# Layer 2's double pairs: the sum that frees a PSUM place is put ahead of the older pair's differences

## The chip, the core and the metric

The kernel runs on one core of a Trainium2 chip. The core has five engines that follow their own instruction queues in order: TensorE (PE, matrix products into PSUM; PEld loads its weights), VectorE (DVE), ScalarE (ACT), GpSimd (POOL) and SyncE (SP, which here only issues DMAs). They wait for each other through semaphores. The metric is the device time of one execution in microseconds (us), the median of several runs.

## What is computed

```python
def _attn_ref(x, w_r, w_i, b_r, b_i):          # x: (2, 3008, 256)
    X = np.fft.rfft(x, axis=1)
    Xr, Xi = X.real, X.imag
    Yr = Xr @ w_r - Xi @ w_i + b_r
    Yi = Xr @ w_i + Xi @ w_r + b_i
    Yr = np.sign(Yr) * np.maximum(np.abs(Yr) - lam, 0.0)
    Yi = np.sign(Yi) * np.maximum(np.abs(Yi) - lam, 0.0)
    return np.fft.irfft(Yr + 1j * Yi, n=x.shape[1], axis=1)

x = _attn_ref(...).reshape(6016, 256)
h = x @ w_in1;  x = (h / (1 + np.exp(-h))) @ w_out1        # layer 1, 256 -> 2048 -> 256
h = x @ w_in2;  y = np.maximum(0.01 * h, h) @ w_out2       # layer 2, 256 -> 2048 -> 256
```

Everything is float32. The spectral part comes first and is no subject here.

## The kernel before, in words

The 6016 tokens stand in the free dimension, in 12 chunks of 512 (the last has 384). Each fp32 operand of a matrix product is split into a high part of fewer bits and a low remainder, and a product is three matmuls (high by low, low by high, high by high). So every value that PE is to read next costs a cast on ACT (the high part, `high`, names `h`, `ha`, `hb`) and a subtraction on DVE or POOL (the remainder, `low`, names `l`, `la`, `lb`).

The 2048 hidden features are 16 blocks of 128, two to a **pair**, 8 pairs p = 0..7 to a chunk. A pair's first product (256 -> 2 x 128 features) goes to PSUM, is activated, and goes through a second product into the accumulators `acc`. The second product uses a scheme with seven instead of eight block products, for which differences of the activated blocks are needed: `t1` (POOL), `t23` and `t4` (DVE).

In layer 2, in chunks 2 to 10 (`FAST`), the odd pairs use such a scheme for the first product too: `unit` computes seven products 1 to 7 of 256 columns in two PSUM places `a` and `b`, one after another. What a place holds is copied away by ACT (`keep`) or summed by DVE with a kept part (`join`) before the next product uses the place again. Product 7 begins `b` anew, so it must wait until the first `join` has read `b`.

An even pair `pr` and the odd pair `fa` behind it are worked on together by `both_pairs`, a **double pair**: 4 to a chunk (p = 0, 2, 4, 6), 36 in all. The order of the calls in `both_pairs` is the order of the instructions in each engine's queue; no scheduler changes it. A double pair also finishes the pairs before it: `one` is the `fa` of the double pair before, `two` its `pr`. PE's order is `pr.first(0)`, products 1 and 2, `pr.first(1)`, products 6 and 7, `two`'s second product in parts "1" and "a", products 5 and 4, `two`'s part "b", product 3, and `one`'s three parts, of which "b" reads `hb` and `lb` of `one`. `make_next` inserts one step of work for the next chunk's input: in p = 0 a load, in p = 2 its split (`xhi`, `xlo`), in p = 4 four sums (`xsum`, two on POOL, then two on DVE), in p = 6 their split (`xs`). At a chunk's end (in p = 0, for the chunk before) `finish` joins the accumulators, with five sums on DVE and two on POOL.

The lines that the texts name: 582 `first`; 599 `activate`; 619 `unit`; 624 `keep`; 627 `join`; 645 `low`; 657 `t1`; 664 `t23`; 671 `t4`; 683 `high`; 690 the second product; 479 `sums_x2`; 751 to 756 `finish`. The sum in question and the two differences:

```python
        def join(self, at_, src, key):
            nc.vector.tensor_tensor(out=quarter(self.f1, at_), in0=self.ph[src], in1=self.ph[key], op=ALU.add)
...
                nc.vector.tensor_tensor(out=v[:, 3:5], in0=b22, in1=v[:, 0:2], op=ALU.subtract)
...
                nc.vector.tensor_tensor(out=u[:, 1280:], in0=u[:, 1024:1280], in1=b2[:, 256:], op=ALU.subtract)
```

`b2` is in PSUM for an even pair and in SBUF (`f1`) for an odd one; `u`, the casts and the kept parts are in SBUF. `high("b")` and `low("b")` of a pair need its `t23` and `t4`; `high("a")` and `low("a")` need its `t1`.

Of the kernel before, what the change touches and what calls it, by code (L numbers as in the profile page):

```python
# [80 lines left out]
def spectral_mlp_kernel(ctx, tc, x, w_r, w_i, b_r, b_i, w_in1, w_out1, w_in2, w_out2, da, ea, dm, out):  # L81
# [695 lines left out]
    def make_next():  # L777
        if todo and (make := todo.pop(0)):
            make()

    def both_pairs(i):

        two, one, pr, fa = pairs[i - 2:i + 2]
        one.high("1")
        one.low("1")
        one.t23()
        pr.first(0)
        one.t4()
        pr.activate(0)
        pr.t1()  # L790
        fa.unit(1, 2)
        fa.keep("p1", "a")
        fa.join(2, "b", "p1")
        one.high("a")
        one.low("a", nc.gpsimd)
        pr.first(1)
        one.high("b")
        one.low("b")
        pr.activate(1)
        fa.unit(6, 7)  # L800
        fa.keep("u2", "a")
        fa.keep("p7", "b")
        two.products("1")
        pr.t23()
        pr.t4()
        two.products("a")
        pr.high("1")
        pr.high("a")
        pr.low("a", nc.gpsimd)
        fa.unit(5, 4)  # L810
        fa.join(1, "a", "p7")
        fa.join(0, "b", "u2")
        pr.low("1")
        if pr.p != 4:
            make_next()
        two.products("b")
        pr.high("b")
        pr.low("b")
        fa.unit(3)
        fa.activate_fast()  # L820
        fa.t1()
        if pr.p == 4:
            make_next()
        for which in "1ab":
            one.products(which)
        one.finish(0)
        one.finish(1)

    for i in range(len(pairs) + 2):
        if i < len(pairs) and (pairs[i].fast or i + 1 < len(pairs) and pairs[i + 1].fast):  # L830
            if not pairs[i].fast:
                if pairs[i].p == 0 and (k := phases.index((2, pairs[i].c)) + 1) < len(phases):
                    todo = ahead(*phases[k])
                both_pairs(i)
            continue
        pr = pairs[i] if i < len(pairs) else None
        one, two = blocks(i - 1), blocks(i - 2)
# [114 lines left out]
```

## Time and profile before

| | |
|---|---|
| median of 3 runs | 1213.45 us (1213.26 to 1213.97) |
| the profiled execution | 1213.22 us, its span 1211.2 us |
| mean granted clock of TensorE | 0.975 |
| busy, share of the span | PE 97%, DVE 71%, ACT 67%, POOL 54% |
| layer 2's 36 double pairs | 742.20 to 1169.40 us of the span |

The span runs from the first to the last instruction. PE's matmuls are pipelined, so a row's duration overlaps the next row; the distance of the starts is what a matmul costs. The granted clock is what the throttle lets TensorE have, as a share of full speed. An idle time in brackets is that of the engine just before the instruction, with what ended it.

### The profile page before, as it was taken

How to read it: one execution, taken by the hardware profiler on the slowest of the kernel's cores; microseconds unless marked ns; L12 is line 12 of the kernel's file. 1: busy time of each engine (PE TensorE's matmuls, PEld its weight loads, DVE VectorE, ACT ScalarE, POOL GpSimd, SP SyncE). 2: the span in 40 equal slices, each digit the busy share in tenths (PEclk: the TensorE clock that was granted, in tenths of full speed). 3: DMA queues.
4: the chain of work that ended last, by engine and by line, in shares of the span. 5: the costliest groups of instructions: out<-in, count | busy, mean ns of one | idle time of the engine just before them, and what ended most of it. 6: DMA issues, size and time to landing. Idle time of an engine off the chain costs nothing.

```text
span 1211.2 us, 21096 instructions
## 1 busy us (share of the span) xinstructions
PE 1169.0 (97%) x7608; PEld 1078.7 (89%) x7608; DVE 860.8 (71%) x1484; ACT 814.4 (67%) x1720; POOL 649.7 (54%) x683
## 2 busy tenths in 40 slices
PE   9999999999999999999999999899899989998998
PEld 9898988889999999999999998888888878888898
DVE  4888865556667666666657788787878787878773
ACT  4888776666666666666657776566666666665674
POOL 0668656534445454544536777565655555555542
PEclk9999999999999999999999999899989999998999
DMA  9445541011121111111101010000100010000000
GB/s 237 123 136 161 157 128 58 13 49 50 35 61 57 40 57 49 47 44 45 36 1 35 32 35 23 32 19 18 35 19 18 18 35 19 18 19 31 19 1 31
DMA packets 36185, 61.80 MB, mean 51 GB/s; under 512 B 3953, under 2 KB 16081, under 8 KB 36081
## 3 DMA queue, kind: packets, MB, share of 16 engines
q1 hardware_dynamic: 35792, 60.28, 16.5%
q8 instruction: 60, 0.98, 0.4%
q14 instruction: 45, 0.36, 0.1%
q10 hardware_dynamic: 288, 0.18, 0.0%
HBM read 41.83 MB, written 18.61 MB: 50 GB/s over the span
## 4 chain that ended last, share of the span: by engine, by line
PE 81%; DVE 9%; ACT 4%; issue 4%; POOL 2%; ACTq 0%; POOLq 0%
PE acc L690 33%; PE ph L582 28%; PE pz L332 5%; PE ph L619 5%; DVE u L664 3%; PE py L361 3%; PE pa L284 2%; PE px L444 2%; DVE l L645 2%; PE pb L384 1%; ACT ha L683 1%; DVE xsum L479 1%; POOL u L657 1%; ACT u L631 1%; DVE f L627 1%
## 5 line engine op out<-in xcount | busy, mean ns | idle before, releaser
L645 POOL TENSOR_TENSOR la<-u,ha 128x512 fp32r<-128x512 f32 (+1 forms) x176 | 230.5, 1310 | 242.5 <-ACT ha L683 242.2
L645 DVE TENSOR_TENSOR lb<-u,hb 128x768 fp32r<-128x768 f32 (+1 forms) x176 | 199.5, 1133 | 191.3 <-ACT hb L683 190.9
L582 PE MATMUL ph<-xhi,winhi 128*128 128x512 f32 (+1 forms) x624 | 188.2, 382 | 0.0
L582 PE MATMUL ph<-xlo,winhi 128*128 128x512 f32 (+1 forms) x624 | 187.9, 381 | 0.0
L582 PE MATMUL ph<-xhi,winlo 128*128 128x512 f32 (+1 forms) x624 | 187.2, 380 | 0.0
L683 ACT CAST hb<-u 128x768 fp32r<-128x768 f32 (+1 forms) x176 | 141.2, 802 | 62.1 <-DVE u L671 59.2
L657 POOL TENSOR_TENSOR u<-u 128x256 f32<-128x256 f32 x160 | 146.6, 916 | 59.5 <-PE ph L619 23.6
L690 PE MATMUL acc<-hb,wlo 128*128 128x256 f32 (+1 forms) x496 | 137.9, 278 | 0.0
L690 PE MATMUL acc<-hb,whi 128*128 128x256 f32 (+1 forms) x496 | 137.6, 277 | 0.0
L690 PE MATMUL acc<-lb,whi 128*128 128x256 f32 (+1 forms) x496 | 137.6, 277 | 0.0
L582 PEld LDWEIGHTS ph<-xhi,winhi 128*128 128x128 f32 x624 | 116.4, 187 | 21.7
L582 PEld LDWEIGHTS ph<-xlo,winhi 128*128 128x128 f32 x624 | 116.4, 187 | 21.3 <-POOL xlo L467 0.3
L683 ACT CAST ha<-u 128x512 fp32r<-128x512 f32 (+1 forms) x176 | 109.0, 619 | 8.6 <-PE acc L690 7.2
L683 ACT CAST h<-ph 128x512 fp32r<-128x512 f32 (+1 forms) x140 | 80.3, 573 | 48.8 <-DVE u L671 30.2
L582 PEld LDWEIGHTS ph<-xhi,winlo 128*128 128x128 f32 x624 | 104.5, 187 | 9.6 <-ACT u L599 0.2
L597 ACT ACTIVATE ph<-ph 128x512 f32<-128x512 f32 (+1 forms) x112 | 64.7, 577 | 63.8 <-PE ph L582 63.8
L690 PE MATMUL acc<-ha,wlo 128*128 128x256 f32 (+1 forms) x352 | 104.0, 295 | 0.0
L690 PE MATMUL acc<-la,whi 128*128 128x256 f32 (+1 forms) x352 | 103.7, 295 | 0.0
L690 PE MATMUL acc<-ha,whi 128*128 128x256 f32 (+1 forms) x352 | 102.8, 292 | 0.0
L690 PE MATMUL acc<-h,wlo 128*128 128x256 f32 (+1 forms) x336 | 99.5, 296 | 0.0
L690 PE MATMUL acc<-h,whi 128*128 128x256 f32 (+1 forms) x336 | 98.3, 293 | 0.0
L690 PE MATMUL acc<-l,whi 128*128 128x256 f32 (+1 forms) x336 | 98.3, 292 | 0.0
(157 smaller groups left out, 3088.5 us busy)
## 6 DMA issues: line engine op xcount, KB each, us to landing
wraw<-in_moe_w_in_dram SPq DMA_DIRECT2D x32, 256.0 KB
wraw<-in_moe_w_out_dram SPq DMA_DIRECT2D x32, 256.0 KB
scr<-bo SPq DMA_DIRECT2D x48, 128.0 KB
scr<-x2o SPq DMA_DIRECT2D x22, 256.0 KB
x2i<-scr SPq DMA_DIRECT2D x22, 256.0 KB
out_dram<-x2o SPq DMA_DIRECT2D x22, 256.0 KB
dmr<-in_dm_dram SPq DMA_DIRECT2D x34, 160.0 KB
bt<-scr SPq DMA_DIRECT2D x14, 384.0 KB
```

The costliest lines, as they stand in the source:

```text
L284: nc.tensor.matmul(pa[h][:, s * 128:(s + 1) * 128], lhsT=xt[c][:, s, h * 128:(h + 1) * 128], rhs=da_sb, start=True, stop=True, skip_group_ ...
L332: nc.tensor.matmul(turned(pz), lhsT=u[:, h, :], rhs=turned(v[:, h].rearrange("p g e -> p (g e)")), start=(n == 0), stop=(n == len(terms) - 1))
L361: nc.tensor.matmul(turned(py), lhsT=u, rhs=turned(v), start=False, stop=(n == len(terms) - 1), skip_group_check=True)
L444: nc.tensor.matmul(px[:, s * PAIR:(s + 1) * PAIR], lhsT=bt[:, s, h * 128:(h + 1) * 128], rhs=ea_sb, start=True, stop=True, skip_group_chec ...
L582: nc.tensor.matmul(turned(ph), lhsT=u[:, h, f % HALF * 128:][:, :128], rhs=turned(v[:, h, :]), start=(i == 0), stop=(i == len(terms) - 1))
L597: nc.scalar.activation(out=out, in_=ph, func=ACTF.Silu)
L619: nc.tensor.matmul(turned(self.ph[dst]), lhsT=u, rhs=turned(m), start=(begin and i == 0), stop=(i == 2), skip_group_check=True)
L645: eng.tensor_tensor(out=lo, in0=src, in1=hi.bitcast(F32), op=ALU.subtract)
L657: nc.gpsimd.tensor_tensor(out=blk(1), in0=blk(0), in1=blk(2), op=ALU.subtract)
L664: nc.vector.tensor_tensor(out=v[:, 3:5], in0=b22, in1=v[:, 0:2], op=ALU.subtract)
L683: nc.scalar.copy(hi, src)
L690: nc.tensor.matmul(turned(dst), lhsT=u, rhs=turned(v), start=(begin and self.p == 0 and i == 0), stop=(end and self.p == NF // 2 - 1 and i ...
```

## The change

Four calls in `both_pairs` for the older pair `one` (`t23`, `t4`, `high("b")`, `low("b")`) move to later places; nothing is added or dropped.

```diff
         two, one, pr, fa = pairs[i - 2:i + 2]
         one.high("1")
         one.low("1")
-        one.t23()
         pr.first(0)
-        one.t4()
         pr.activate(0)
         pr.t1()
         fa.unit(1, 2)
         fa.keep("p1", "a")
         fa.join(2, "b", "p1")
+        one.t23()
+        one.t4()
         one.high("a")
         one.low("a", nc.gpsimd)
         pr.first(1)
-        one.high("b")
-        one.low("b")
         pr.activate(1)
         fa.unit(6, 7)
         fa.keep("u2", "a")
         fa.keep("p7", "b")
+        one.high("b")
         two.products("1")
         pr.t23()
         pr.t4()
@@
         fa.unit(5, 4)
         fa.join(1, "a", "p7")
         fa.join(0, "b", "u2")
+        one.low("b")
         pr.low("1")
         if pr.p != 4:
             make_next()
```

On DVE the rows of a double pair with p = 2 read so in the kernel before, from `low("1")` of `one` to `low("b")` of `pr` (`f_` and `l_`, `h_` with a number are the tiles `f1`, `l1`, `h1`; `ph` is PSUM; `kept` is what `keep` copied):

```order
L645 TENSOR_TENSOR l_12659<-f_12577,h_12658 128x512
L664 TENSOR_TENSOR u<-f_12577,u 128x512
L671 TENSOR_TENSOR u<-u,f_12577 128x256
L627 TENSOR_TENSOR f_12722<-ph,kept 128x256
L645 TENSOR_TENSOR lb<-u,hb 128x768
L664 TENSOR_TENSOR u<-ph,u 128x512
L671 TENSOR_TENSOR u<-u,ph 128x256
L627 TENSOR_TENSOR f_12722<-ph,kept 128x256 x2
L645 TENSOR_TENSOR l_12717<-ph,h_12716 128x512
L467 TENSOR_TENSOR xlo<-x2i,xhi 128x512
L645 TENSOR_TENSOR lb<-u,hb 128x768
```

and in the changed kernel, at the same place of the queue:

```order
L645 TENSOR_TENSOR l_12659<-f_12575,h_12658 128x512
L627 TENSOR_TENSOR f_12720<-ph,kept 128x256
L664 TENSOR_TENSOR u<-f_12575,u 128x512
L671 TENSOR_TENSOR u<-u,f_12575 128x256
L664 TENSOR_TENSOR u<-ph,u 128x512
L671 TENSOR_TENSOR u<-u,ph 128x256
L627 TENSOR_TENSOR f_12720<-ph,kept 128x256 x2
L645 TENSOR_TENSOR lb<-u,hb 128x768
L645 TENSOR_TENSOR l_12715<-ph,h_12714 128x512
L467 TENSOR_TENSOR xlo<-x2i,xhi 128x512
L645 TENSOR_TENSOR lb<-u,hb 128x768
```

The first `join` moved up by two rows, and the first `lb` (that of `one`) moved down by five, behind the two later joins. On ACT the rows of a double pair in the kernel before, from `activate(0)` to `high("b")` of `pr`:

```order
L599 ACTIVATE u<-ph 128x2x256
L624 COPY kept<-ph 128x256
L683 CAST ha<-u 128x512
L683 CAST hb<-u 128x768
L599 ACTIVATE ph<-ph 128x512
L624 COPY kept<-ph 128x256 x2
L683 CAST h_12571<-ph 128x512
```

and in the changed kernel:

```order
L599 ACTIVATE u<-ph 128x2x256
L624 COPY kept<-ph 128x256
L683 CAST ha<-u 128x512
L599 ACTIVATE ph<-ph 128x512
L624 COPY kept<-ph 128x256 x2
L683 CAST hb<-u 128x768
L683 CAST h_12569<-ph 128x512
```

The cast `hb` of `one` moved down behind `activate(1)` and the two copies. The rows of PE and POOL keep their order.

## Rows read from the trace of the kernel before

**Rows 1.** The page, busy time of each engine over the span.

```profile
PE 1169.0 (97%) x7608; PEld 1078.7 (89%) x7608; DVE 860.8 (71%) x1484; ACT 814.4 (67%) x1720; POOL 649.7 (54%) x683
```

**Rows 2.** The waits of PE: us in total, times, longest us.

```profile
PE ph L619 <- DVE f L627: 37.4, 18, 2.4
```

**Rows 3.** Windows: us, busy us of PE, PEld, DVE, ACT, POOL; granted clock; DMA.

```profile
742.20:1169.40 427.20, 389.71 (x2702) 368.82 (x2701) 341.15 (x476) 277.72 (x569) 239.19 (x197) 0.93 0.06 22
...
902.60:906.30 3.70, 3.68 (x18) 3.68 (x19) 2.07 (x3) 2.18 (x6) 0.77 (x1) 0.54 0.00 0
```

**Rows 4.** PE's timeline: start, duration, instruction; starts of double pairs, and line 619.

```profile
746.88 0.61 PE L619 MATMUL ph<-xs,ws 128*128 128x256 f32 x3 [0.44 <-DVE f L627]
...
896.44 0.63 PE L582 MATMUL ph<-xhi,winlo 128*128 128x512 f32 x2
...
902.62 1.01 PE L619 MATMUL ph<-xs,ws 128*128 128x256 f32 x3 [2.24 <-DVE f L627]
...
910.48 0.61 PE L582 MATMUL ph<-xhi,winlo 128*128 128x512 f32 x2
...
913.85 0.85 PE L619 MATMUL ph<-xs,ws 128*128 128x256 f32 x6
...
919.43 0.28 PE L690 MATMUL acc<-lb,whi 128*128 128x256 f32 x1
...
920.35 0.60 PE L582 MATMUL ph<-xhi,winlo 128*128 128x512 f32 x2
...
926.48 1.01 PE L619 MATMUL ph<-xs,ws 128*128 128x256 f32 x3 [2.23 <-DVE f L627]
...
934.38 0.60 PE L582 MATMUL ph<-xhi,winlo 128*128 128x512 f32 x2
...
944.38 0.60 PE L582 MATMUL ph<-xhi,winlo 128*128 128x512 f32 x2
```

**Rows 5.** DVE's timeline from a double pair with p = 2 on.

```profile
896.85 0.75 DVE L751 TENSOR_TENSOR x2o<-x2o,acc 128x256 f32<-128x256 f32 x2 [0.68 <-ACT x2o L747]
...
898.51 1.18 DVE L645 TENSOR_TENSOR l<-f,h 128x512 fp32r<-128x512 f32 x1
899.61 1.76 DVE L664 TENSOR_TENSOR u<-f,u 128x512 f32<-128x512 f32 x1
901.40 0.83 DVE L671 TENSOR_TENSOR u<-u,f 128x256 f32<-128x256 f32 x1
902.15 0.41 DVE L627 TENSOR_TENSOR f<-ph,kept 128x256 f32<-128x256 f32 x1
903.13 1.05 DVE L645 TENSOR_TENSOR lb<-u,hb 128x768 fp32r<-128x768 f32 x1 [0.56 <-ACT hb L683]
...
916.61 0.75 DVE L627 TENSOR_TENSOR f<-ph,kept 128x256 f32<-128x256 f32 x2
...
935.70 0.68 DVE L664 TENSOR_TENSOR u<-f,u 128x512 f32<-128x512 f32 x1
```

**Rows 6.** ACT's timeline in the same double pair.

```profile
902.27 0.83 ACT L683 CAST hb<-u 128x768 fp32r<-128x768 f32 x1 [2.80 <-DVE u L671]
```

**Rows 7.** POOL's timeline in that double pair, and around the start of p = 6.

```profile
899.10 1.72 POOL L756 TENSOR_TENSOR x2o<-x2o,u 128x512 f32<-128x512 f32 x1
900.78 1.17 POOL L657 TENSOR_TENSOR u<-u 128x256 f32<-128x256 f32 x1
901.91 1.45 POOL L645 TENSOR_TENSOR la<-u,ha 128x512 fp32r<-128x512 f32 x1
...
917.99 1.28 POOL L645 TENSOR_TENSOR la<-u,ha 128x512 fp32r<-128x512 f32 x1 [3.16 <-ACT ha L683]
919.37 1.31 POOL L657 TENSOR_TENSOR u<-u 128x256 f32<-128x256 f32 x1
920.64 1.42 POOL L479 TENSOR_TENSOR xsum<-x2i 128x256 f32<-128x256 f32 x2
...
922.61 0.79 POOL L657 TENSOR_TENSOR u<-u 128x256 f32<-128x256 f32 x1 [0.55 <-ACT u L599]
```

## The prediction

> **What bounds the kernel now.** I read the page first: the matmul engine PE is busy for 97% of the span [rows 1], so time can only come out of what PE loses. The list of PE's waits has one entry of weight: PE stands at line 619 for a DVE instruction of line 627, 18 times, 37.4 us together [rows 2]. Line 627 is `join`, the sum that reads PSUM place `b` before product 7 may overwrite it. Then I read PE's timeline [rows 4]. All the waits lie in layer 2's 36 double pairs, which run from 742.20 to 1169.40, 427.2 us [rows 3]. I count times in a double pair from the start of its `first(0)`, written +x. Two hindered ones start at 896.44 and 920.35 and last 14.04 and 14.03; two unhindered ones start at 910.48 and 934.38 and last 9.87 and 10.00, mean 9.94. 36 x 9.94 = 357.8, so 69.4 us are lost. The first double pair waits 0.44 us and costs 1.1; the other 17 cost 4.0 each. A chunk has four double pairs, p = 0, 2, 4, 6. Hindered are p = 2 (behind the five DVE sums of `finish`; 9 chunks) and p = 6 (behind the two DVE sums of `sums_x2`; 8 chunks, since the last fast chunk has none).
>
> Why 4.0, when PE idles 2.24? After the wait PE runs from 902.60 to 906.30 at a granted clock of 0.54, close to the lower of its levels (1.2 GHz), against 0.93 over all double pairs [rows 3]; 3.7 x 0.46 = 1.7 us more. The wait of 0.44 us at 746.88 was followed by matmuls at the usual pace [rows 4].
>
> Next, DVE and POOL side by side [rows 5, 7]. In p = 2 the DVE queue before `join` is: sums of `finish` from 896.85, `low("1")` to 899.69, `t23` to 901.37, `t4` to 902.23, `join` from 902.15; product 7 starts 0.47 after that, at 902.62. `t23` takes 1.76 here and 0.68 at 935.70. The ends explain it: POOL's line 756 ends at 900.82, DVE's `t23` at 901.37, POOL's `t1` at 901.95, DVE's `t4` at 902.23, POOL's `la` at 903.36, DVE's `lb` at 904.18. DVE instructions with both inputs in SBUF and POOL instructions run strictly in turns. A turn lasts 0.55 (512 columns), 0.28 (256) or 0.82 (768) on DVE, and 0.58 (256) or 1.13 (512) on POOL. For DVE instructions with a PSUM input I assume that they take no turn; the two joins from 916.61 show no stretch.
>
> The Trainium skill (SBUF — State Buffer, section Who interferes with whom) says the same: a DVE instruction with two SBUF inputs and a POOL instruction that reads SBUF exclude each other through one shared read port, for the whole instruction. It speaks against the full gain: by unhindered DVE durations the sum would be 1145, by turns 1173 (both worked out below from rows). The trace agrees, to about 0.1 us.
>
> **The change, part by part.** No instruction is added or dropped; PE's and POOL's orders stay, and no DMA moves. On DVE `join` comes ahead of `t23` and `t4` of `one`, and `lb` of `one` goes behind the two later joins. On ACT the copy `hb` of `one` goes behind `activate(1)` and two `keep`s; before, ACT stood 2.80 us for `t4` in front of it [rows 6], and `activate(1)` and the `keep`s, which PE's product 5 and DVE's differences need, stood behind it. They no longer wait for DVE, so ACT's edit costs nothing.
>
> p = 2: up to `low("1")` everything is as before, so `join` runs at +3.17 (899.61) in place of +5.71, and product 7 could start at +3.64. Its unhindered place is +3.7 (six matmuls from 913.85, in a double pair from 910.48). The wait goes. `t23` had to wait for POOL's line 756 until 900.82 anyway, so the 0.41 of `join` lies under that and `t4` still ends at +5.79. The two differences of `pr` (1.1 together, then 0.75 for the two joins at 916.61) bring DVE to +7.5, and `lb` of `one` to +8.36. PE's first matmul that reads it stands at +8.95 (919.43), so 0.6 us remain. The new wait costs nothing under that cover; without it, 1 us per us.
>
> From there I carry the turns forward. `la` of `pr` 9.49, DVE's `xlo` 10.06, POOL's `xlo` 11.19, `lb` of `pr` 12.01, `t1` of `fa` 12.59, `low("1")` of the next 13.16. The next double pair, p = 4, began at 9.94, so `low("1")` ends at its +3.2 and `join` starts in time, with only 0.1 to spare.
>
> p = 4: `t1` +3.8, `t23` +4.35, `la` +5.5, `t4` +5.8, differences +6.85, joins +7.5, `lb` of `one` +8.4. `la` of `pr` follows the last difference by 1.3 us now (joins 916.61, `la` 917.99), so it gets the turn after: 9.5; `lb` of `pr` 10.35; `t1` of `fa` 10.9. That is +0.97 of p = 6. Now it ends at 920.68, +0.33 [rows 7]. So DVE and POOL arrive 0.6 us late at `sums_x2`, because the stall in p = 2 no longer lets them catch up.
>
> p = 6: now the POOL sums end at 922.06, 1.38 after that `t1`; then both DVE sums get their turns before POOL's next `t1` (its row starts at 922.61), and `low("1")` gets its turn behind that `t1`, ahead of `la`. 0.6 later, the POOL sums end at +2.35, one DVE sum +2.65, `t1` +3.25, the second DVE sum +3.55, `la` +4.7, `low("1")` +5.25. `join` starts at +5.17 and product 7 at +5.65, where now it is +6.13 (926.48). The point is 0.45 us: had p = 4 ended that much earlier, `low("1")` would come before `la`, and the wait would fall to about 0.3.
>
> After such a stall p = 0 begins clean, as p = 0 and p = 4 do now. So I take: p = 2 saves 9 x 4.0 = 36, p = 6 saves 8 x 0.5 = 4. Does PE still slow down after an idle time of 1.7? Bounds: the 0.44 us wait did not slow it, waits of 2.0 and more did; 1.7 is nearer to these, so I take the slow clock; without it another 8 x 1.7 = 14 go. Against the profiled execution's 1213.22 (0.2 below the median) the sum is 1213.2 - 40 = 1173.
>
> **Rivals.** (1) *Both waits go.* The turns are then shorter, or PE is slower by half a microsecond per chunk, so that `low("1")` in p = 6 precedes `la`. For: 0.45 us decides, over a chain of some 25 instructions. Against: each turn is one of the trace's. 1213.2 - 68 = 1145, with left-over waits of up to 0.8 per chunk 1152.
>
> (2) *DVE paces every double pair.* DVE is busy 341.15 of 427.2 us, 9.48 per double pair, and PE needs 9.94; POOL's share would rise from 0.56 (239.19) to some 0.64 in the shorter time, and the turns lost with it. For: only 0.46 us per double pair is left. Against: part of the 9.48 is the stretch in the stalls themselves. With 0.5 us lost per double pair 1145 + 18 = 1163, with the slow clock in half of the chunks' places about 1190.
>
> (3) *Slower.* `lb` of `one` now ends at 904.18, some 5 us before PE reads it at the end of that double pair (910.48 less 1.0), and after the change 0.6 us before. If POOL takes one more turn ahead of it (1.13), PE waits 0.5 in each of 36, 18 us, not enough. If it loses two turns, w = 1.7 and PE waits 61 us: 1213 - 40 + 61 = 1234, and more with the slow clock. It decides from w = 1.1 (40 / 36). Queued behind it on DVE are `low("1")`, `xlo` and `lb` of `pr`, and `fa`'s first activation, which now writes a buffer that `lb` of `one` must have read. Against: POOL has nothing ready between +5.5 and +8.4.
>
> (4) *It does not do what it says*: `join` waits for something else than its place in the queue, and the time stays at 1213. Against: at 902.15 it starts 0.08 before `t4` ends, back to back, while PE had products 1 and 2 behind it, and product 6 too, by 900.38 (902.62 less the 2.24 of idle time).
>
> **How the numbers follow.** A measurement of this kernel tells 0.2%, 2.4 us. Forecast (the wait goes from p = 2 and stays in p = 6): 0.52, own range 1158 (no slow clock) to 1181 (p = 6 as long as now and small waits). Rival 1: 0.22, 1145 to 1158. Rival 2: 0.15, 1160 to 1195. Rival 4, or a wait that only moves: 0.05. Slower: 0.06. The range 1146 to 1186 leaves out about 2 in 10. Faster by over 0.2%: 0.52 + 0.22 + 0.15 + 0.01 = 0.90; within: 0.04; slower: 0.06.
>
> **What would show it.** In the list of PE's waits the entry at line 619 falls from 18 to about 8, all in p = 6, some 1.7 us each; p = 2 lasts 9.9 to 10.1; in p = 2 `join` ends before `t23`. In p = 4 `t1` of `fa` ends about 1.0 after the next `first(0)`, and in p = 6 POOL's `la` comes before `low("1")`. ACT's 2.80 us wait before `hb` is gone or no longer holds `activate(1)`. A clock below 1 is left only behind p = 6. I am wrong if no wait is left (rival 1), if PE waits at line 690 for `lb` (rival 3), or if p = 2 still stalls.

## The result, and the profile after

The changed kernel takes 1161.36 us (median of 4 runs, 1160.87 to 1161.74) against 1213.68 for the kernel before in the same comparison: a ratio of 0.9569 [0.9552, 0.9586], 52 us less. The forecast was 1173 with a range of 1146 to 1186. The profiled execution lasts 1160.99 us, its span 1159.0.

The page of the changed kernel, engines, answering to [rows 1]:

```profile
PE 1141.4 (98%) x7608; PEld 1052.2 (91%) x7608; DVE 867.5 (75%) x1484; ACT 816.7 (70%) x1720; POOL 668.5 (58%) x683
```

PE's waits, answering to [rows 2]:

```profile
PE ph L619 <- DVE f L627: 12.7, 8, 1.6
```

Windows, with the columns of [rows 3]: the 36 double pairs, then the 3.7 us behind one of the eight waits that are left:

```profile
742.09:1117.22 375.13, 362.38 (x2702) 342.66 (x2701) 348.51 (x476) 279.99 (x569) 257.55 (x197) 1.00 0.08 25
903.57:907.27 3.70, 3.70 (x32) 3.70 (x32) 3.24 (x7) 2.74 (x6) 0.35 (x1) 1.00 0.08 32
```

The double pairs shrank from 427.20 to 375.13 us. That is 52.1 of the 52.2 us by which the span shrank; next to nothing came or went elsewhere. Eighteen waits became eight. The granted clock over the double pairs rose from 0.93 to 1.00, and behind the wait that ends at 903.57 it is 1.00 too, where behind the one of 902.62 in [rows 3] it was 0.54.

PE's timeline of one chunk, answering to [rows 4]: the starts of p = 2, 4, 6, 0 and 2, product 7 in p = 2 and p = 6, and the first read of `lb` of `one` in p = 2:

```profile
878.01 0.60 PE L582 MATMUL ph<-xhi,winlo 128*128 128x512 f32 x2
...
881.46 0.85 PE L619 MATMUL ph<-xs,ws 128*128 128x256 f32 x6
...
887.22 0.28 PE L690 MATMUL acc<-lb,whi 128*128 128x256 f32 x1
...
888.14 0.61 PE L582 MATMUL ph<-xhi,winlo 128*128 128x512 f32 x2
...
898.08 0.62 PE L582 MATMUL ph<-xhi,winlo 128*128 128x512 f32 x2
...
903.57 0.63 PE L619 MATMUL ph<-xs,ws 128*128 128x256 f32 x3 [1.58 <-DVE f L627]
...
909.90 0.40 PE L582 MATMUL ph<-xhi,winlo 128*128 128x512 f32 x1
...
919.87 0.60 PE L582 MATMUL ph<-xhi,winlo 128*128 128x512 f32 x2
```

The lengths follow from the starts: p = 2 lasts 10.13 (before 14.04), p = 4 9.94, p = 6 11.82 (before 14.03), p = 0 9.97. In p = 2 products 6 and 7 run on as one group of six matmuls, without idle time. In p = 6 the wait is still there, 1.58 in place of 2.23, and the matmuls behind it run at the usual pace (0.63 for three; 1.01 in [rows 4]).

DVE's timeline from p = 2 to p = 6 of that chunk, answering to [rows 5]:

```profile
880.05 1.19 DVE L645 TENSOR_TENSOR l<-f,h 128x512 fp32r<-128x512 f32 x1
881.17 0.41 DVE L627 TENSOR_TENSOR f<-ph,kept 128x256 f32<-128x256 f32 x1
881.50 1.43 DVE L664 TENSOR_TENSOR u<-f,u 128x512 f32<-128x512 f32 x1
882.96 0.84 DVE L671 TENSOR_TENSOR u<-u,f 128x256 f32<-128x256 f32 x1
...
885.44 0.95 DVE L645 TENSOR_TENSOR lb<-u,hb 128x768 fp32r<-128x768 f32 x1
...
889.99 1.22 DVE L645 TENSOR_TENSOR l<-f,h 128x512 fp32r<-128x512 f32 x1
...
899.68 1.81 DVE L479 TENSOR_TENSOR xsum<-x2i,xsum 128x256 f32<-128x256 f32 x2 [1.33 <-POOL xsum L479]
901.42 1.75 DVE L645 TENSOR_TENSOR l<-f,h 128x512 fp32r<-128x512 f32 x1
903.10 0.41 DVE L627 TENSOR_TENSOR f<-ph,kept 128x256 f32<-128x256 f32 x1
```

ACT's cast `hb` of `one` in p = 2, answering to [rows 6], and POOL's timeline around the start of p = 6, answering to [rows 7]:

```profile
883.84 0.84 ACT L683 CAST hb<-u 128x768 fp32r<-128x768 f32 x1 [1.04 <-DVE u L671]
```

```profile
897.52 1.43 POOL L657 TENSOR_TENSOR u<-u 128x256 f32<-128x256 f32 x1
898.91 1.44 POOL L479 TENSOR_TENSOR xsum<-x2i 128x256 f32<-128x256 f32 x2
900.36 0.86 POOL L657 TENSOR_TENSOR u<-u 128x256 f32<-128x256 f32 x1
901.18 1.45 POOL L645 TENSOR_TENSOR la<-u,ha 128x512 fp32r<-128x512 f32 x1
```

Counted from the starts of the double pairs: in p = 2 `join` starts at +3.16 (forecast +3.17), `t4` ends at +5.79 (+5.79), `lb` of `one` ends at +8.38 (+8.36) and is first read at +9.21. `low("1")` of p = 4 ends at +13.20 (+13.16). In p = 6 `t1` of `fa` ends at +0.87 (+0.97; before +0.33), POOL's `la` gets its turn ahead of `low("1")`, `join` starts at +5.02 (+5.17) and product 7 at +5.49 (+5.65).

So two things need an answer: why eight waits of 1.6 us are not followed by a slow clock, and what the three parts of the edit did, since the prediction gave the gain to one of them.

### The profile page after: what moved, and what is told of

The parts are those of the page before. It is cut to its first block, busy times and chain, and to the rows that moved or that the text cites. A ratio compares the mean times of both kernels' runs of the same rounds, so it can differ in the third digit from the quotient of the medians.

```text
span 1159.0 us, 21096 instructions
## 1 busy us (share of the span) xinstructions
PE 1141.4 (98%) x7608; PEld 1052.2 (91%) x7608; DVE 867.5 (75%) x1484; ACT 816.7 (70%) x1720; POOL 668.5 (58%) x683
## 4 chain that ended last, share of the span: by engine, by line
PE 82%; DVE 9%; issue 4%; POOL 2%; ACT 2%; DMA 0%; SPq 0%; ACTq 0%; POOLq 0%
PE acc L690 33%; PE ph L582 31%; PE pz L332 6%; PE ph L619 4%; PE py L361 3%; PE px L444 2%; PE pa L284 2%; DVE u L664 2%; DVE l L645 2%; PE pb L384 1%; DVE f L627 1%; POOL u L657 1%; DVE lb L645 1%; POOL la L645 1%; DVE xsum L479 1%
## 5 line engine op out<-in xcount | busy, mean ns | idle before, releaser
L645 POOL TENSOR_TENSOR la<-u,ha 128x512 fp32r<-128x512 f32 (+1 forms) x176 | 245.4, 1395 | 199.7 <-ACT ha L683 195.2
L645 DVE TENSOR_TENSOR lb<-u,hb 128x768 fp32r<-128x768 f32 (+1 forms) x176 | 193.7, 1100 | 154.6 <-ACT hb L683 154.0
L657 POOL TENSOR_TENSOR u<-u 128x256 f32<-128x256 f32 x160 | 150.9, 943 | 32.0 <-ACT u L597 22.2
L690 PE MATMUL acc<-ha,wlo 128*128 128x256 f32 (+1 forms) x352 | 99.1, 282 | 0.0
L690 PE MATMUL acc<-ha,whi 128*128 128x256 f32 (+1 forms) x352 | 98.8, 281 | 0.0
L690 PE MATMUL acc<-la,whi 128*128 128x256 f32 (+1 forms) x352 | 98.8, 281 | 0.0
L690 PE MATMUL acc<-h,wlo 128*128 128x256 f32 (+1 forms) x336 | 94.7, 282 | 0.0
L597 ACT ACTIVATE u<-ph 128x512 f32<-128x512 f32 (+1 forms) x80 | 47.1, 588 | 67.1 <-PE ph L582 65.2
L690 PE MATMUL acc<-l,whi 128*128 128x256 f32 (+1 forms) x336 | 93.6, 278 | 0.0
L690 PE MATMUL acc<-h,whi 128*128 128x256 f32 (+1 forms) x336 | 93.5, 278 | 0.0
```

The lines of the kernel that those rows point to most:

```text
L597: nc.scalar.activation(out=out, in_=ph, func=ACTF.Silu)
L645: eng.tensor_tensor(out=lo, in0=src, in1=hi.bitcast(F32), op=ALU.subtract)
L657: nc.gpsimd.tensor_tensor(out=blk(1), in0=blk(0), in1=blk(2), op=ALU.subtract)
L690: nc.tensor.matmul(turned(dst), lhsT=u, rhs=turned(v), start=(begin and self.p == 0 and i == 0), stop=(end and self.p == NF // 2 - 1 and i ...
```

## The experiments

Diffs are against the changed kernel; ratios are against the kernel before. No experiment leaves work out; the kernels with the sum made again write the same values twice or three times. My theory was that of the prediction: `join`'s place in the queue is the gain, turns between DVE and POOL keep it late in p = 6, and the wait that is left brings a slow clock or not. The rivals were that the later cast `hb` and the later subtraction `lb` do the work (the headings call these two the copies), and that DVE paces every double pair.

### The sum alone, and the copies alone

The sum alone (the cast and the subtraction back where they were, the two differences behind the sum):

```diff
         pr.first(1)
+        one.high("b")
+        one.low("b")
         pr.activate(1)
...
         fa.keep("p7", "b")
-        one.high("b")
...
         fa.join(0, "b", "u2")
-        one.low("b")
```

> Only the sum and the two differences of the older pair change places; the cast hb and the remainder lb stand where they stood before the change (hb ahead of activate(1), lb ahead of the even pair's differences). Theory A (both edits are needed: with t4 now later, hb holds activate(1) and the two keeps on ACT until t4 is done, so PE waits at product 5 instead of product 7): t4 ends at +5.8 in p = 2 and about +5.7 in p = 4, hb to +6.6, keeps to +7.7, against +5.4 for product 5, a wait of some 2 us in p = 2 and p = 4, with the slow clock 2 to 4 us each; about 1161 + 9 x 2 x (2 to 4) = 1197 to 1233, PE's waits at line 619 then end on ACT's line 624. Rival B (the sum's place alone gives the gain, hb and lb are side dishes): 1158 to 1166, PE's waits as in the changed kernel, 8 of 1.6 us.

The copies alone (both differences back):

```diff
         one.low("1")
+        one.t23()
         pr.first(0)
+        one.t4()
...
         fa.join(2, "b", "p1")
-        one.t23()
-        one.t4()
```

> Only hb and lb of the older pair move to the later places; the two differences stand ahead of the sum as before the change. Theory A (the wait at product 7 hangs on the sum's place in DVE's queue): the sum still starts at +5.7 in p = 2 and about +5.6 in p = 6, the 17 waits of some 2.2 us with the slow clock stay, 1205 to 1214. Rival B (the gain is ACT's, which no longer stands 2.8 us for t4): 1160 to 1175 and no waits in p = 2.

The sum alone: 1223.23 us, ratio 1.0074 [1.0059, 1.0089]. The copies alone: 1223.01 us, 1.0070 [1.0055, 1.0086]. Each half by itself is 9 us slower than the kernel before. PE's waits, first with the sum alone, then with the copies alone:

```profile
PE ph L619 <- ACT kept L624: 50.6, 36, 1.9
PE ph L619 <- DVE f L627: 9.4, 8, 1.5
```

```profile
PE ph L619 <- DVE f L627: 48.5, 26, 3.0
```

With the sum alone the old wait is gone but for p = 6, and a new one stands in every double pair, for ACT. With the copies alone I expected at most the time before; the old waits grew instead, to 2.2 to 3.0 in p = 2 and p = 6, and small ones of 0.2 to 0.4 stand in some of the other double pairs. DVE's timeline of that kernel, the later joins in p = 2:

```profile
908.90 0.76 DVE L627 TENSOR_TENSOR f<-ph,kept 128x256 f32<-128x256 f32 x2 [2.80 <-PE ph L619]
```

DVE stands 2.80 us for PE ahead of these joins, and `lb` of `one` is made only behind them, from 909.58 on. In the kernel before it was made ahead of them (903.13 in [rows 5]). So its work comes out of DVE's idle time into the busy stretch behind, and that is a likely reason for the longer waits; no run tests it.

### Which of the two copies

Only ACT's cast back where it was:

```diff
         pr.first(1)
+        one.high("b")
         pr.activate(1)
...
         fa.keep("p7", "b")
-        one.high("b")
```

> As the changed kernel, but on ACT the cast hb of the older pair stands ahead of activate(1) and the two keeps, as before the change; DVE's order is that of the changed kernel. Theory A (ACT's edit is needed: hb holds the keeps until t4, and t4 is later now): PE waits at product 5 for line 624 in nearly every double pair, 1.5 to 1.9 us as in the run with the sum alone, 1210 to 1223. Rival B (that run's waits came from lb on DVE, not from hb on ACT): 1161 to 1170.

Only DVE's subtraction back, ahead of `pr`'s differences:

```diff
         one.high("b")
+        one.low("b")
         two.products("1")
...
         fa.join(0, "b", "u2")
-        one.low("b")
```

> As the changed kernel, but the remainder lb of the older pair stands in DVE's queue behind the first sum and the older pair's differences, ahead of the even pair's differences, as before the change. Theory A (lb's later place is what keeps DVE from standing idle for hb, which ACT now makes behind the keeps): DVE stands 0.5 to 1 us for hb in each double pair, falls behind by so much, and PE's waits grow or appear in p = 4: 8 to 17 waits, 1165 to 1190. Rival B (lb's place is free, the 0.6 us of cover shows that nothing hangs on it): 1160 to 1163.

The cast back in its place: 1213.61 us (10 runs), ratio 0.9998 [0.9989, 1.0008], so that all 52 us are gone again. ACT's timeline and PE's in p = 6 of that kernel:

```profile
878.72 0.83 ACT L683 CAST hb<-u 128x768 fp32r<-128x768 f32 x1 [2.92 <-DVE u L671]
879.45 0.58 ACT L599 ACTIVATE ph<-ph 128x512 f32<-128x512 f32 x1
879.97 0.63 ACT L624 COPY kept<-ph 128x256 f32<-128x256 f32 x2
```

```profile
880.38 0.61 PE L619 MATMUL ph<-xs,ws 128*128 128x256 f32 x3 [1.49 <-ACT kept L624]
```

ACT stands for `t4`, now later than before, with `activate(1)` and both `keep`s queued behind; PE's product 5 needs the place that the first `keep` copies away. There are 36 such waits, 51.1 us.

The subtraction back in its place: 1222.84 us, ratio 1.0071 [1.0054, 1.0088]. I had expected 1165 to 1190; that missed. PE's waits of that kernel, then the timelines of ACT, DVE and PE in p = 6 (PE's second row is in the p = 0 behind it):

```profile
PE ph L619 <- DVE f L627: 59.9, 47, 1.9
```

```profile
881.75 0.37 ACT L624 COPY kept<-ph 128x256 f32<-128x256 f32 x1 [1.56 <-PE ph L619]
882.14 0.84 ACT L683 CAST hb<-u 128x768 fp32r<-128x768 f32 x1
```

```profile
883.01 0.96 DVE L645 TENSOR_TENSOR lb<-u,hb 128x768 fp32r<-128x768 f32 x1 [0.90 <-ACT hb L683]
...
884.94 0.75 DVE L627 TENSOR_TENSOR f<-ph,kept 128x256 f32<-128x256 f32 x2
```

```profile
885.41 0.38 PE L619 MATMUL ph<-xhi,ws 128*128 128x256 f32 x1 [0.59 <-DVE f L627]
...
897.14 0.38 PE L619 MATMUL ph<-xhi,ws 128*128 128x256 f32 x1 [1.51 <-DVE f L627]
```

Of the 47 waits 36, with 47.2 of the 59.9 us, are at product 3 (`xhi,ws`), one in every double pair; at product 7 stand the eight of p = 6 and three small ones in p = 2. The first of the two later joins must read place `a` before product 3 may use it. DVE stands for the late `hb`, then makes `lb`, and `pr`'s differences and both joins are queued behind. So what `lb` passes in the change counts: on DVE it goes behind four instructions, the two differences of `pr` and the two joins ("moved down by five" above is wrong). From 864.32 to 912.48 four double pairs take 48.16, 12.04 each, where four of the changed kernel's take 41.85 (868.05 to 909.90).

### The wait that is left in p = 6

In p = 6, `la` of `one` on DVE:

```diff
-        one.low("a", nc.gpsimd)
+        one.low("a", nc.vector if pr.p == 6 else nc.gpsimd)
```

> As the changed kernel, but in p = 6 the remainder la of the older pair is made by DVE (behind t4) in place of POOL; nothing else moves. Theory A (low("1") in p = 6 stands 1.13 us for POOL's la, by turns): without that turn low("1") ends about 1.1 earlier, at +4.0, the wait at product 7 falls from 1.6 to about 0.5 us, 1161.4 - 8 x 1.1 = 1152.5, range 1151 to 1156, although DVE has 0.6 us more to do. Rival B (DVE's own queue is what makes the sum late, POOL does not matter): waits stay at 1.6 us or grow, 1161 to 1168.

In p = 6, the sum also ahead of `low("1")` of `one`:

```diff
-        one.low("1")
+        if pr.p != 6:
+            one.low("1")
...
         fa.join(2, "b", "p1")
+        if pr.p == 6:
+            one.low("1")
```

> As the changed kernel, but in p = 6 alone the first sum also goes ahead of low("1") of the older pair on DVE. Theory A (what is left in p = 6 is the sum's place behind low("1"), which loses its turn to POOL's la): the sum starts behind the second DVE sum of sums_x2, at about +3.3, product 7 at about +3.8, the 8 waits fall from 1.6 to at most 0.2 us: 1161.4 - 8 x 1.5 = 1149, range 1147 to 1153. Rival B (DVE as a whole is the bound, so the loss comes back at another place, at line 690 for l or lb, or at product 7 in p = 0): 1157 to 1162.

In p = 4, `la` of `one` on DVE, behind `t4` of `pr`:

```diff
-        one.low("a", nc.gpsimd)
+        if pr.p != 4:
+            one.low("a", nc.gpsimd)
...
         pr.t4()
+        if pr.p == 4:
+            one.low("a")
```

> As the changed kernel, but in p = 4 the remainder la of the older pair is made by DVE (behind the even pair's t4) in place of POOL; p = 6 is untouched. Theory A (the wait in p = 6 comes from turns lost in p = 4, which make t1 of the odd pair and the sums of sums_x2 late): without POOL's la the older pair's t4 in p = 4 stands no 1.13 us, t1 of the odd pair ends at about +0.3 of p = 6 as in the kernel before, low("1") in p = 6 comes ahead of la, its wait falls from 1.6 to about 0.3 us: 1161.4 - 8 x 1.3 = 1151, range 1149 to 1154. Rival B (the wait in p = 6 is made in p = 6 alone, by the two DVE sums and POOL's two sums, whatever came before): 8 waits of 1.4 to 1.6 us stay, 1160 to 1163.

Without POOL's `la` in p = 6: 1152.69 us, 0.9496 [0.9482, 0.9510]. PE's waits of that kernel:

```profile
PE ph L619 <- DVE f L627: 3.9, 8, 0.5
```

The eight waits fall from 1.6 to 0.5, that is by 1.1, one POOL turn of 512 columns as the prediction read it (1.13). The Trainium skill (SBUF — State Buffer, section Who interferes with whom) names the shared read port behind this; the trace agrees as to the exclusion, at 1.1 us for the avoided turn, and does not show the port itself.

With `la` off POOL in p = 4, a double pair earlier: 1151.55 us, 0.9487 [0.9473, 0.9501], the lowest median of all. Seven of the eight waits are 0.2 to 0.3, one remained. PE's timeline, an earlier chunk and that one:

```profile
857.99 0.61 PE L619 MATMUL ph<-xs,ws 128*128 128x256 f32 x3 [0.32 <-DVE f L627]
...
899.77 0.49 PE L619 MATMUL ph<-xs,ws 128*128 128x256 f32 x2 [1.46 <-DVE f L627]
```

POOL's timeline there: `t1` of `pr` and `la` of `one` in p = 6, in the earlier chunk and in that one:

```profile
856.05 1.00 POOL L657 TENSOR_TENSOR u<-u 128x256 f32<-128x256 f32 x1 [0.34 <-ACT u L599]
857.01 1.72 POOL L645 TENSOR_TENSOR la<-u,ha 128x512 fp32r<-128x512 f32 x1
...
896.68 0.74 POOL L657 TENSOR_TENSOR u<-u 128x256 f32<-128x256 f32 x1 [0.28 <-ACT u L599]
897.46 1.37 POOL L645 TENSOR_TENSOR la<-u,ha 128x512 fp32r<-128x512 f32 x1
```

And DVE's `low("1")` in the same two places:

```profile
856.37 1.23 DVE L645 TENSOR_TENSOR l<-f,h 128x512 fp32r<-128x512 f32 x1
...
897.62 1.76 DVE L645 TENSOR_TENSOR l<-f,h 128x512 fp32r<-128x512 f32 x1
```

In the earlier chunk `low("1")` ends at 857.60 and `la` at 858.73, one POOL turn later; in the other `la` ends at 898.83 and `low("1")` at 899.38, one DVE turn later. The wait has two values here, not a range, and which of the two it is turns on little: the `t1` of `fa` that p = 4 hands on ends 0.53 after the start of p = 6 in the one (854.32 - 853.79) and 0.59 in the other (895.01 - 894.42); +0.3 had been expected. In the seven chunks with the short wait POOL's sums of `sums_x2` end 1.83 to 1.92 after that start, in this one 1.97. That a lag carried over from p = 4 decides is what the prediction said; it put the point 0.45 below its forecast of +0.97, at +0.52, and here it lies between +0.53 and +0.59.

With the sum moved ahead once more in p = 6, the wait there goes (two small ones in p = 2 are left, 0.6 us together), but the time is 1154.85 us, 0.9511 [0.9497, 0.9525], no better than with `la` on DVE and between the two expected ranges. PE's timeline in p = 2 of that kernel; then windows, of a whole chunk and from the first `finish` sum of p = 2 to the last `lb` of p = 4; and the latter in the changed kernel:

```profile
879.46 1.18 PE L619 MATMUL ph<-xs,ws 128*128 128x256 f32 x6
```

```profile
865.99:906.94 40.95, 40.78 (x303) 38.23 (x302) 38.76 (x55) 31.17 (x65) 28.61 (x23) 1.00 0.08 27
876.80:896.74 19.94, 19.89 (x150) 18.67 (x149) 19.80 (x28) 15.55 (x32) 14.40 (x12) 1.00 0.07 28
```

```profile
878.39:898.35 19.96, 19.96 (x151) 18.90 (x151) 19.82 (x28) 15.45 (x32) 14.38 (x11) 1.00 0.07 28
```

DVE (third of the engines) is busy for 19.8 of 19.9 us from p = 2 to p = 4, in both; its busy time includes what its instructions stand for POOL's turns. What PE gains in p = 6 brings it earlier to p = 2, where DVE has no slack: products 6 and 7 take 1.18 in place of 0.85, and the double pair starts at 876.01 and ends at 886.53, 10.52. The 0.33 are idle times of PE too short for the list of waits, which begins at 0.15.

Two combinations asked whether the gains add. In p = 6, the sum ahead of `low("1")` as above, and `la` on DVE behind the later joins:

```diff
-        one.low("a", nc.gpsimd)
+        if pr.p != 6:
+            one.low("a", nc.gpsimd)
...
         fa.join(0, "b", "u2")
+        if pr.p == 6:
+            one.low("a")
         one.low("b")
```

> As the changed kernel, but in p = 6 the first sum goes ahead of low("1"), and la of the older pair is made by DVE behind the later joins. Theory A (both delays of p = 6, product 7 by the sum and product 3 by the join that frees place a, go): p = 6 lasts 10.0, p = 2 10.2 to 10.5, 1148 to 1152. Rival B (DVE's 0.6 us more makes lb of the older pair late for PE, or the next chunk's p = 2 late): 1153 to 1158.

And the two diffs above for p = 6's sum and p = 4's `la` together:

> As the run with la on DVE in p = 4, and in p = 6 the first sum ahead of low("1"). Theory A: the rest of the wait in p = 6 goes too, p = 6 lasts 10.0, 1147 to 1151, below both runs with one of the two. Rival B (DVE is the bound, what is saved in p = 6 is lost in the next p = 0 and p = 2, as p = 2 went from 10.13 to 10.5 in the run with the sum first alone): 1151 to 1156.

They came to 1153.34 us (0.9499 [0.9483, 0.9514]) and 1152.89 us (0.9495 [0.9481, 0.9510]). Both expectations missed by 1 to 2 us, and the rival held: the waits are nearly gone, and it is no faster than one of the edits alone. In all five of these kernels a chunk takes 40.7 to 41.0 us, and DVE is busy for 38.4 to 38.8 of them; its longest idle time there is 1.32, for POOL's `xsum` in p = 6. PE alone would need four times 9.94, 39.8. So DVE's queue, turns included, is the likely limit that they share. No run gave DVE less to do, so this is argued, not shown.

### The clock behind a wait

The sum of p = 6 made twice, which lengthens the wait; then three times, with 2 in place of 1:

```diff
         fa.join(2, "b", "p1")
+        for _ in range(1 if pr.p == 6 else 0):
+            fa.join(2, "b", "p1")
```

> As the changed kernel, but in p = 6 the first sum is made twice, the second time with the same result, so that product 7 waits 0.34 us longer: idle times of about 1.94 us in 8 places. Theory A (TensorE's granted clock falls after an idle time somewhere between 1.6 and 2.0 us, as behind every wait of 1.97 us and more in the kernel before): clock below 1 behind some or all of these waits, 1161.4 + 8 x (0.34 + 1.7) = 1178, or between 1164 and 1178 when only some do. Rival B (it is not the idle time but what else the long waits had): clock 1.0, 1164.

> As the run with two sums, but three: idle times of about 2.3 us in 8 places. Theory A (length of the idle time): the slow clock behind all 8, 1161.4 + 8 x (0.68 + 1.7) = 1180, range 1177 to 1184. Rival B (something else): clock 1.0, 1167.

The sum made twice: 1173.76 us, 0.9668 [0.9652, 0.9684]. Three times: 1179.63 us, 0.9719 [0.9704, 0.9733]. The waits are 1.98 to 2.06 and 2.47 to 2.53, some 0.45 longer for each added sum, where 0.34 was expected. Windows of the 3.7 us behind two of the eight waits with the sum twice (both 2.06 long), and behind two with the sum three times (2.47 and 2.48):

```profile
908.07:911.77 3.70, 3.70 (x18) 3.70 (x19) 1.99 (x4) 1.99 (x4) 0.00 (x0) 0.54 0.00 0
...
1039.55:1043.25 3.70, 3.70 (x32) 3.70 (x33) 3.25 (x7) 2.74 (x5) 0.34 (x1) 1.00 0.01 3
```

```profile
779.79:783.49 3.70, 3.70 (x32) 3.70 (x33) 3.25 (x7) 2.74 (x5) 0.34 (x1) 1.00 0.00 0
822.70:826.40 3.70, 3.70 (x19) 3.70 (x20) 1.99 (x4) 2.12 (x4) 0.00 (x0) 0.56 0.00 0
```

The clock is the third column from the end. It fell behind five of eight waits of 2.0 (0.54 to 0.69) and behind seven of eight of 2.5 (0.56 to 0.62); in the changed kernel, where the waits are 1.55 to 1.61, it is 1.00 behind all eight. With the sum three times the idle time grew by 20.0 - 12.7 = 7.3 us, and the time by 18.3; the other 11 us are seven slow stretches of 1.6. Both times lie in the ranges of theory A, but the length of the idle time alone does not decide: with three sums all eight were to be slow, and with two sums waits of the same length fall on both sides.

## Why the prediction was right, and where it was not

**The mechanism held.** The wait goes from p = 2 and stays in p = 6, for the reason given: DVE and POOL take turns, and p = 4 hands its lag on. The schedule carried forward over two double pairs was met within 0.16 us at each of the points of DVE and POOL, and at product 7, and taking one POOL turn away shortened the wait by that turn. The p = 2 term was 9 x 4.0 = 36; p = 2 now lasts 10.13 for 14.04, so 9 x 3.9 = 35.

**The term that was mis-sized** is the slow clock in p = 6. "1.7 is nearer to these, so I take the slow clock": behind none of the eight waits did the granted clock fall. The term was 8 x 0.5 = 4; measured is 14.03 - 11.82 = 2.21 each, 17.7 in all; of the 2.21, 0.65 is the shorter wait and the rest the clock. The 14 us that the prediction named for this case take 1173 to 1159, and 1161 was measured. The end of the forecast's own range, "1158 (no slow clock)", was the better centre; the bounds, 0.44 without and 2.0 with a slow clock, left it open.

**What the total hid** is the step "so ACT's edit costs nothing", and the same reasoning for `lb`. In the changed kernel PE waits for neither, but the prediction priced the two as side changes and gave the gain to the sum's place. The runs show three parts that work only together: without the cast's move 1213.6, without the subtraction's 1222.8, without the sum's 1223.0. With `t4` later, whatever waits for it must go behind what PE needs next. For ACT the text has that (the `keep`s), but not its price without the move, 52 us; for DVE it never named the later joins as what frees place `a` for product 3.

**Rivals.** (1) "Both waits go" did not happen here, but the point from which it decides was real: 1.1 us of POOL's turns taken away brings 1151.5 to 1152.7, inside its 1145 to 1158. (2) The time of 1161.4 lies in this rival's range too, 1160 to 1195, so the total does not tell. The lengths do: DVE does not pace every double pair, since p = 0 and p = 4 last 9.94 to 9.97; but it is without slack from p = 2 to p = 4, and that probably stops five different repairs between 1151.5 and 1154.9. (3) `lb` did not stall PE: it ends 0.8 us before it is read. The argument against this rival, "POOL has nothing ready between +5.5 and +8.4", was wrong: in p = 2 POOL makes `la` of `one` until +6.95, while DVE's instructions read PSUM, and its next `la` starts at +8.14, when `lb` already had its turn. (4) The change did what it says.

**Signs.** As announced: 8 waits, all in p = 6; p = 2 10.1 long; `join` ahead of `t23`; `t1` at +0.87. "A clock below 1 is left only behind p = 6" was the one that failed: it is left nowhere in the double pairs. ACT still waits ahead of `hb`, 1.04, but PE has no wait for ACT in its list.

## What to carry to other kernels

When an instruction is moved ahead in an in-order queue, list for each of the passed ones who waits for it on the other engines, and what stands behind that waiting instruction: here a cast on ACT and a subtraction on DVE had to move too, or the whole gain was lost or more. Price each part of an edit as if it were left out, even where its own cost is nothing. Where two engines share turns, carry the schedule forward by the measured lengths of turns, over more than one stage; it was good to 0.16 us here.

## What the runs showed of the hardware that was not expected

The length of a wait alone does not say whether PE runs slower behind it. In the kernel with the cast back in its place, waits of one length in p = 2 fall on both sides; windows behind one of 1.85 and one of 1.86:

```profile
808.17:811.87 3.70, 3.70 (x18) 3.70 (x19) 3.35 (x7) 2.51 (x6) 1.51 (x1) 0.54 0.01 2
856.75:860.45 3.70, 3.70 (x32) 3.70 (x33) 3.67 (x7) 2.91 (x6) 1.51 (x2) 1.00 0.02 4
```

With the copies alone a wait of 2.73 that ended at 858.29 was followed by 1.00, and one of 2.79 that ended at 905.11 by 0.60. Of waits up to 1.61 in p = 6 of the changed kernel none was followed by a fall. What else decides stays open. Nor do many short waits slow the clock much: with the sum alone, 44 waits, 60.0 us together and none over 1.92, leave a mean granted clock of 0.996 over the span. That kernel is 61.9 us slower than the changed one, and 47.3 us of it (60.0 - 12.7) are added idle time at these waits.
